# Reordering work at the group boundary of a fused linear-attention and gated-MLP kernel: one pair fetched per period, Erf behind the mean, the x split in two pieces, weights' parts behind the copy of k^T v

## The chip, the cores and the metric

The kernel runs on one core of a Trainium2 chip. The metric is the device time of one execution in microseconds (us); the kernel before takes 943.47 us (median of three runs, 943.17 to 945.06). A profiled execution of it spans 943.4 us, so times read in the trace can be compared with the metric directly.

## The reference, cut to what matters

```python
# q, k, v: (8, 8, 576, 64); w_in: (512, 2048); w_out: (2048, 512)
kv  = einsum('bhsd,bhse->bhde', k, v)             # k^T v, 64x64 for each head
out = einsum('bhsd,bhde->bhse', q, kv)            # linear attention, no softmax
rms = sqrt(mean(out * out, axis=-1) + 1e-6)
x   = (out / rms * g_norm) -> (4608, 512)         # tokens x (heads * head_dim)
h   = x @ w_in                                    # 4608 x 2048
g   = h * erf(softplus(h))
y   = g @ w_out                                   # 4608 x 512
```

## The kernel before

**Tiles and stages.** The 4608 tokens are worked in nine groups T of 512: the first 512 rows of each of the eight batches (T = 0 to 7), and the 64 rows left of each of the eight as group 8. The 2048 hidden columns are 16 units of 128, and four units make a *period*; a group has four periods, b = 0 to 3. Groups 0 and 1 form a first stage in which the weights are also converted and cut into parts. From group 2 on, the loop over m (line 1007) runs the periods, with T, b = divmod(m, 4).

**What a product is.** From group 2 on both matrix products work on numbers cut in parts: a rounded upper part, the remainder, and a scaled combination of both. `product` (line 663) therefore issues 12 matmuls of 128x512 for one result: eight into the bank `n_ps` (for each of four blocks k, the upper form and then the lower one) and four into the bank `m_ps`. The two banks are joined when they are read: ScalarE copies `n_ps` scaled into `h` (line 1057), then VectorE adds `m_ps` (line 649). `pair_of_banks` hands out three pairs of banks in turn, so a product waits until the product three before it has been read.

**A period.** In order: four `hidden` products u0 to u3 (x times w_in, for the units of this period), then four `result` products r0 to r3 (g times w_out, for the gate values of the period before; one for each 128 tokens). Around them stand the gate's steps. ScalarE takes Softplus of each `h` (line 1072), then Erf of two halves (line 1078); VectorE multiplies h by it (line 1101); in the next period ScalarE makes the upper part of g (`cut_upper`, which is line 609 in the profile) and VectorE the two lower ones (`cut_lower`, lines 612 and 615). VectorE also adds each result into `e` (lines 644 and 649).

**Attention in between.** While period (T, b) runs, the attention of group T+1 is worked for head pair p = b. `attention` returns it as a list of pieces, and the tuple `places` (lines 1022 to 1031) says where each is issued: 0 is the period's start, 1 to 4 come after u0 to u3, 5 to 8 after r0 to r3. The pieces of a group above 2 (`fused`) are: a first one, empty but for one pair; `visit` with `halve` and `keep_tail`; `loads`; `mean`; `norm`; `split`.

- `visit` (459): TensorE multiplies q by k^T v, and also turns q and works k^T v of the *next* pair; ScalarE squares the result (492) and copies the turned q (344, in `turned`); `tails_kept` (352) copies the last rows of q on VectorE (358) for every second pair; `halve` (517) cuts the squares in two; `keep_tail` keeps the last rows (498) and, by `kv_kept`, k^T v (364 and 371).
- `mean` (524): two pairs of short matmuls (537 and 538), then Ln, Exp and Square on ScalarE (552 to 554). They need another activation table than Softplus and Erf, so they bring a table load.
- `norm` (558): three VectorE operations (560, 563, 572) that give x.
- `split` (581): the upper part of x on ScalarE (609), the two others on VectorE (612 and 615), into `x_forms`, which u0 of the next group reads.
- `loads` (585): q, k and v of a later pair, through the queue of SyncE, into a pool of two buffers for each. In a fused group it fetches the pair three ahead, whose buffers are the ones that this visit has just read; the first fused visit fetches two pairs.

The engines take their work in the order of the code. At the *turn* of a group (b = 3) the last pair's `split` must be done before u0 of the next group can end: the last two of u0's eight `n_ps` matmuls read it.

**The weights.** The parts of w_in and w_out lie in device memory and are streamed in again for each group, 768 KB a unit (`load_parts`, line 801), through the same SyncE queue. `FETCH` (line 1004) gives the places of these loads; w_in has four buffers, so a load waits for the unit four before it. In the first stage `w_upper` and `w_lower` (lines 682 and 698) cut the weights; `w_lower` runs two VectorE operations for each unit at the head of a step (lines 876 and 877), and `keep_prepared`, which brings k^T v of the prepared pair from its bank to `bd_kv` (364 and 371), comes after it, in `steps[f + 1][0]`.

Of the kernel before, what the change touches and what calls it, by code (L numbers as in the profile page):

```python
# [43 lines left out]
AF = mybir.ActivationFunctionType  # L44
# [16 lines left out]
def kernel(  # L61
# [200 lines left out]
    def weights():  # L262

        w_next("split")
        w_next("join")
        w_next("load")
# [126 lines left out]
    def keep_prepared():  # L393
        kept.pop()()

    def attention(T, p, pools=None):

        st = {}

# [59 lines left out]
        def visit():  # L459


            qT, tail = ready.pop((T, p))
            at = st["at"] = at_tile()
            x = halves_of(qT)
            for a, i, o in ((0, 0, 0), (0, 1, 1), (1, 0, 1), (1, 1, 0)):
                nc.tensor.matmul(  # L466
                    at[rows_of[o], a, 0 : 2 * P],
                    lhsT=bd[rows_of[i], a * D : a * D + D],
                    rhs=x[rows_of[i], a],
                    start=True,  # L470
                    stop=True,
                )
            for s in rows_of:
                nc.tensor.matmul(
                    at[s, 0, 2 * P : 2 * P + R], lhsT=bd[s, 0:D], rhs=tail[s], start=True, stop=True
                )
            st["o"] = at[:, :, 0 : 2 * P]
            st["next"] = fused and then[0] < B
            if st["next"]:
                ps = pair_of_banks("q0_ps", "q1_ps")  # L480
                kvs = list(kv_products(*then, at, crossed=True))
                turns = list(turn_products(*then, ps))
                while kvs or turns:
                    for some in (turns, kvs):
                        for product_ in some[:4]:
                            product_()  # L486
                        del some[:4]
            if fused:
                st["sq"] = x_new.tile([P, G], FP32, name="sq", tag="x")
            else:  # L490
                st["sq"] = qT
            nc.scalar.activation(two(st["sq"]), st["o"], AF.Square)
            if st["next"]:
                qT = turned(*then, ps)
                tails_kept(*then, ps, qT)

        def keep_tail():
            nc.vector.tensor_copy(
                out=x_last[:, p, T * R : T * R + R], in_=st["at"][:, 0, 2 * P : 2 * P + R]
            )  # L500
            if st["next"]:
                kv_kept(*then, st["at"])

        def apply():
# [53 lines left out]
        def norm():  # L558
# [19 lines left out]
                op1=ALU.mult,  # L578
            )

        def split():
            if T >= FIRST:
                thirds(st.pop("x"), *(form[:, p] for form in x_forms[T]))

        def loads():
            if not fused or (T, p) == (FIRST + 1, 0):
                load_pair(T * NP + p + 2)
            if fused:
                load_pair(T * NP + p + 3)

        if T == 0:
            return products, apply, halve, mean, norm
# [8 lines left out]
            pieces = ((prepare_,), (visit,), (halve, keep_tail, loads))  # L601
        else:
            pieces = ((prepare_, loads), (visit,), (keep_tail,))
        return (*(partial(chain, *group) for group in pieces), mean, norm, split)


    def upper(x, high):
# [20 lines left out]
    def thirds(x, high, low, both):  # L628
        upper(x, high)
        lower(x, high, low, both)  # L630
# [182 lines left out]
    def pieces_of(T):  # L813


        steps = [([], [], []) for _ in range(FC)]
        for p in range(NP):
            products, apply, halve, mean, norm, split = attention(T, p)
            f = (BATCH - 1) * (p + 1) if T < FIRST else BATCH * p

            steps[f][2 if T == FIRST or p == 1 else 1].append(products)
            steps[f + 1][0].append(keep_prepared)
            steps[f + 1][1].append(apply)
            steps[f + 2][0].append(halve)
            with_erf = (f + 2) % BATCH == BATCH - 1

            place = 2 if T < FIRST and p == 0 else 1
            steps[f + 2][place].append(partial(mean, table=not with_erf))
            steps[f + 3][0].append(norm)
            steps[min(f + 4, FC - 1)][0].append(split)  # L830
        return steps
# [27 lines left out]
    for n in range(FIRST * FC + 1):  # L859
# [10 lines left out]
        if T < FIRST:  # L870
            if f == 0:
                steps = pieces_of(T + 1)

            if due(0 if n == 2 * (BATCH - 1) else 1):
                weights()
            for key in list(w_new)[:2]:
                w_lower(*key)
            for piece in steps[f][0]:
                piece()
# [127 lines left out]
    for m in range(first_batch, batches + 1):  # L1007
        T, b = divmod(m, NB)
        todo = []
        if T + 1 < NG:  # L1010
            todo = list(attention(T + 1, b))
            if b == 0:
                side = late_r if T % 2 == FIRST % 2 else late
                forms = side.tile([P, 3, KC, G], FP32R, name=f"x_forms{(T + 1) % 2}")
                x_forms[T + 1] = [forms[:, i] for i in range(3)]

        def piece():
            if todo:
                todo.pop(0)()


        places = (0, 2, 3, 5, 6, 8)
        if T + 1 == B:
            places = (0, 0, 0, 5, 6, 7)
            if b == NB - 1:


                places, todo[3] = (0, 0, 0, 4, 6, 7), partial(todo[3], table=False)
                todo[5] = partial(chain, todo[5], softplus_table)
        elif b == NB - 1:  # L1030
            places = (0, 2, 3, 5, 6, 7)

        def pieces(place):
            while todo and places[-len(todo)] <= place:
                todo.pop(0)()

        def fetch(place):
            for which in FETCH[place].split():
                load_parts(which, 1)


        to_last = m == B * NB - 1
        pieces(0)
        g, done = g_next, len(g_next)
        g_next = []
        if m < batches:

            pool, tag = (acc, "e") if m % 2 else (wide, "b")
            h = pool.tile([P, BATCH, G], FP32, name="h", tag=tag)
            s = gate_r.tile([P, BATCH, G], FP32, name="s", tag="s")  # L1050
        for i in range(BATCH):
            if m < batches:
                n_ps, m_ps = hidden(T, b * BATCH + i)
            fetch(i)

            def evacuate():
                nc.scalar.activation(h[:, i], n_ps, AF.Copy, scale=SHIFT - 1.0)  # L1057
                add(h[:, i], m_ps)


            early_copy = i == 0 and m == B * NB
            if early_copy:
                evacuate()
            if i == 0:
                for half in range(done, 2):
                    g.append(cut_upper(old_h, half))
            if i == 0 and not done:
                cut_lower(old_h, 0, g[0])
            if m < batches:
                if not early_copy:  # L1070
                    evacuate()
                nc.scalar.activation(s[:, i], h[:, i], AF.Softplus)  # L1072
            if i == BATCH - 1:
                cut_lower(old_h, 1, g[1])
            pieces(i + 1)
        if m < batches:
            for i in range(2):
                nc.scalar.activation(part(s, i), part(s, i), AF.Erf)  # L1078
            if len(todo) < 2:
                softplus_table()  # L1080
        T2, b2 = divmod(m - 1, NB)
        w = [w_now["out", b2 * BATCH + f].pop(0).bitcast(FP32R) for f in range(BATCH)]
        for j in range(J):
            cuts = 2 if m == batches and j == J - 1 else 1
            result(T2, b2, j, g, w, cuts)
            fetch(BATCH + j)
            if b2 == NB - 1:
                e = es.pop(j)
                if cuts == 1:
                    store(T2, j, e)  # L1090
            if j == 1 and m == batches - 1:
                cut_lower(h, 0, g_next[0])

            if m >= batches - 1:
                due_halves = (j,) if j < 2 and m < batches else ()
            else:
                due_halves = range(2) if j == (2 if to_last else 1) else ()
            if to_last:
                pieces(BATCH + 1 + j)
            for half in due_halves:  # L1100
                nc.vector.tensor_tensor(  # L1101
                    out=part(h, half), in0=part(h, half), in1=part(s, half), op=ALU.mult
                )
            if j == 0 and m == batches - 1:
                g_next.append(cut_upper(h, 0))
            pieces(BATCH + 1 + j)
        old_h = h
# [33 lines left out]
```

## Time and profile before

| what | value |
|---|---|
| time, median of 3 | 943.47 us |
| span of the profiled execution | 943.4 us |
| TensorE matmul busy | 920.1 us (98%) |
| VectorE busy | 728.8 us (77%) |
| ScalarE busy | 603.1 us (64%) |
| moved by DMA | 259.99 MB, mean 276 GB/s |
| a product of 12 matmuls, start to start | 2.72 us |
| a period in groups 3 to 6 | 24.3 to 24.4 us; 25.1 to 25.7 us where it begins at a turn |

Busy time of a matmul is a modelled span: one 128x512 matmul is shown with about 390 ns while the next starts 227 ns after it. So small stalls vanish inside busy time, and the distance from one product's start to the next is the better measure of what TensorE loses. An idle time stands in the profile with what ended it, the releaser.

### The profile page before, as it was taken

What the parts mean: (1) busy time and instruction counts of PE and PEld (TensorE: products, weight loads), DVE (VectorE), ACT (ScalarE), POOL (GpSimd) and SP (SyncE); (2) the same over time, 40 slices, a digit from 0 to 9 for tenths busy, and PEclk for the clock granted to TensorE, in tenths of its full rate; (3) what the DMA queues carried; (4) which work ended last, traced back from release to release, by engine and by line L of the source; (5) the groups of instructions that cost most, each with busy time, mean ns of one, the idle gap of its engine ahead of it and who ended that gap; (6) DMA issues with size and microseconds to landing.
All of it is one profiled execution on the core that took longest, in us unless ns stands there. A gap on an engine that the chain in (4) does not pass through costs nothing.

```text
span 943.4 us, 15388 instructions
## 1 busy us (share of the span) xinstructions
PE 920.1 (98%) x5998; PEld 685.3 (73%) x5998; DVE 728.8 (77%) x1074; ACT 603.1 (64%) x830; POOL 2.4 (0%) x10
## 2 busy tenths in 40 slices
PE   6999999999999999999999999999999999999998
PEld 4444445565687887888788878887888788888886
DVE  2788848788576888888878887888888878776677
ACT  3877666677665666666656666666666666665552
POOL 1000000000000000000000000000000000000000
PEclk9999999999999999999999999999999999999999
DMA  9866406888589998899888988998877678778872
GB/s 258 287 209 205 135 1 253 322 342 333 200 288 333 330 335 296 289 321 329 272 296 311 320 290 303 333 309 278 284 318 261 247 264 342 275 281 324 321 271 56
DMA packets 108271, 259.99 MB, mean 276 GB/s; under 512 B 43992, under 2 KB 66856, under 8 KB 108200
## 3 DMA queue, kind: packets, MB, share of 16 engines
q1 hardware_dynamic: 106488, 256.73, 76.8%
q10 hardware_dynamic: 1648, 2.29, 0.8%
q8 instruction: 47, 0.77, 0.3%
q14 instruction: 24, 0.20, 0.1%
q0 software_dynamic: 64, 0.00, 0.0%
HBM read 224.40 MB, written 34.60 MB: 275 GB/s over the span
## 4 chain that ended last, share of the span: by engine, by line
PE 71%; DVE 16%; ACT 6%; DMA 4%; issue 2%; SPq 0%; DVEq 0%; ACTq 0%
PE n_ps L671 35%; PE m_ps L671 17%; PE o_ps L727 8%; PE h_ps L907 4%; DVE e L649 3%; DVE h L1101 2%; DVE e L644 2%; DVE h L649 2%; PE at_ps L466 1%; DVE g_forms L612 1%; DMA w_in_parts<-w_in 1%; PE at_ps L486 1%; DMA k_sb<-in_k_dram 1%; DVE x L572 1%; DVE u L563 1%
## 5 line engine op out<-in xcount | busy, mean ns | idle before, releaser
L671 PE MATMUL n_ps<-x_forms,w_in_parts 128*128 128x512 f32 x896 | 227.8, 395 | 6.2 <-DVE x_forms L612 3.9
L671 PE MATMUL n_ps<-w_out_parts,g_forms 128*128 128x512 f32 x928 | 232.0, 392 | 0.0
L671 PEld LDWEIGHTS n_ps<-w_out_parts,g_forms 128*128 128x128 f32 x928 | 172.9, 188 | 37.1 <-issue 1.9
L671 PEld LDWEIGHTS n_ps<-x_forms,w_in_parts 128*128 128x128 f32 x896 | 167.1, 188 | 45.0 <-DVE x_forms L612 5.6
L1072 ACT ACTIVATE s<-h 128x512 f32<-128x512 f32 x112 | 70.8, 632 | 190.4 <-DVE h L649 190.3
L649 DVE TENSOR_TENSOR h<-m_ps,h 128x512 f32<-128x512 f32 x116 | 79.9, 689 | 90.8 <-ACT h L1057 60.3
L671 PE MATMUL m_ps<-w_out_parts,g_forms 128*128 128x512 f32 (+1 forms) x468 | 124.3, 388 | 0.0
L671 PE MATMUL m_ps<-x_forms,w_in_parts 128*128 128x512 f32 x448 | 120.5, 391 | 0.0
L727 PE MATMUL o_ps<-w_out_sb,h_sb 128*128 128x512 f32 x224 | 101.8, 597 | 0.2 <-DVE h_sb L857 0.2
L671 PEld LDWEIGHTS m_ps<-w_out_parts,g_forms 128*128 128x128 f32 x468 | 87.5, 188 | 18.5
L671 PEld LDWEIGHTS m_ps<-x_forms,w_in_parts 128*128 128x128 f32 x448 | 84.7, 189 | 17.8
L649 DVE TENSOR_TENSOR e<-m_ps,e 128x512 f32<-128x512 f32 (+1 forms) x117 | 80.3, 687 | 14.5 <-PE m_ps L671 3.8
L727 PEld LDWEIGHTS o_ps<-w_out_sb,h_sb 128*128 128x128 f32 x224 | 41.4, 190 | 44.8 <-issue 42.2
L1057 ACT ACTIVATE h<-n_ps 128x512 f32<-128x512 f32 x112 | 66.1, 590 | 10.4 <-PE n_ps L671 10.2
L615 DVE SCALAR_TENSOR_TENSOR g_forms<-g_forms 128x1024 fp32r<-128x1024 f32 x58 | 71.1, 1225 | 2.0
L612 DVE TENSOR_TENSOR g_forms<-h,g_forms 128x1024 fp32r<-128x1024 f32 x58 | 70.5, 1216 | 0.1
L609 ACT ACTIVATE g_forms<-h 128x1024 fp32r<-128x1024 f32 x58 | 58.4, 1048 | 15.1 <-PE m_ps L671 11.1
L1101 DVE TENSOR_TENSOR h<-h,s 128x1024 f32<-128x1024 f32 x56 | 65.9, 1216 | 0.0
L907 PE MATMUL h_ps<-xT,w_in_sb 128*128 128x512 f32 x144 | 64.8, 596 | 0.5 <-DVE w_in_sb L245 0.5
L644 DVE SCALAR_TENSOR_TENSOR e<-n_ps,e 128x512 f32<-128x512 f32 x88 | 60.1, 683 | 3.5 <-PE n_ps L671 3.5
L108 ACT ACT_TABLE_LOAD x44 | 56.5, 1283 | 0.7
L1078 ACT ACTIVATE s<-s 128x1024 f32<-128x1024 f32 x56 | 56.3, 1053 | 0.3
(128 smaller groups left out, 1023.4 us busy)
## 6 DMA issues: line engine op xcount, KB each, us to landing
w_out_parts<-w_out SPq DMA_DIRECT2D x116, 768.0 KB
w_in_parts<-w_in SPq DMA_DIRECT2D x112, 768.0 KB
w_in<-w_new SPq DMA_DIRECT2D x16, 768.0 KB
q_sb<-in_q_dram SPq DMA_DIRECT2D x32, 256.0 KB
w_raw<-in_moe_w_in_dram SPq DMA_DIRECT2D x16, 512.0 KB
w_raw<-in_moe_w_out_dram SPq DMA_DIRECT2D x8, 1024.0 KB
out_dram<-e SPq DMA_DIRECT2D x32, 256.0 KB
k_sb<-in_k_dram SPq DMA_DIRECT2D x28, 287.5 KB
```

The source lines that it names most:

```text
L108: nc.scalar.preload_act_table_set("softplus")
L609: nc.scalar.activation(high, x, AF.Copy, scale=1.0 + 2.0**-13)
L612: nc.vector.tensor_tensor(out=low, in0=x, in1=high.bitcast(FP32), op=ALU.subtract)
L615: nc.vector.scalar_tensor_tensor(out=both, in0=low.bitcast(FP32), scalar=SHIFT, in1=high.bitcast(FP32), op0=ALU.mult, op1=ALU.add,)
L644: nc.vector.scalar_tensor_tensor(out=out_, in0=ps, scalar=scale, in1=out_, op0=ALU.mult, op1=ALU.add)
L649: nc.vector.tensor_tensor(out=out_, in0=ps, in1=out_, op=ALU.add)
L671: nc.tensor.matmul(ps[:, cols], lhsT=weights(form, k), rhs=moving(form, k)[:, cols], start=(form == forms[0] and k == 0), stop=(form == fo ...
L727: nc.tensor.matmul(o_ps[j], lhsT=g[:, j * P : j * P + P], rhs=w_out_sb[:, f, :], start=(f == 0), stop=last,)
L907: nc.tensor.matmul(plain[i], lhsT=w_in_sb[:, i % FC, c], rhs=xT[T][:, c, :], start=(c == 0), stop=(c == KC - 1),)
L1057: nc.scalar.activation(h[:, i], n_ps, AF.Copy, scale=SHIFT - 1.0)
L1072: nc.scalar.activation(s[:, i], h[:, i], AF.Softplus)
L1101: nc.vector.tensor_tensor(out=part(h, half), in0=part(h, half), in1=part(s, half), op=ALU.mult)
```

## The change

The diff has four parts.

1. *One pair fetched per period.* `loads` fetches the pair two ahead, never three, and the first fused visit no longer fetches two pairs. Its target buffers are those of the visit before, so the load need not wait for the matmuls just issued.
2. *The turn of a group* (b = 3, five times). `mean` moves from after r0 to before Erf (place 4), without a table load of its own for Softplus; only the first half's Erf comes right after it, the second half's Erf and the Softplus table come after r0; `norm` moves from place 6 to 5; `split` is cut into `split_upper` (place 5) and `split_lower` (place 6); the product h times s moves from r1 to r2. At the first period of each group from 3 on, the copy of u0 from its banks comes ahead of `cut_upper` and `cut_lower` (before, only in group 8).
3. *The tails of q behind halve.* `tails_kept` moves from `visit` into `keep_tail`.
4. *Weights' parts behind k^T v's copy.* In the first stage `keep_prepared` runs ahead of `w_lower`.

```diff
@@ attention @@
             nc.scalar.activation(two(st["sq"]), st["o"], AF.Square)
             if st["next"]:
-                qT = turned(*then, ps)
-                tails_kept(*then, ps, qT)
+                st["turned"] = ps, turned(*then, ps)
         def keep_tail():
             ...
-            if st["next"]:
+            if st.get("next"):
+                tails_kept(*then, *st.pop("turned"))
                 kv_kept(*then, st["at"])
...
+        def split_upper():
+            if T >= FIRST:
+                upper(st["x"], x_forms[T][0][:, p])
+
+        def split_lower():
+            if T >= FIRST:
+                lower(st.pop("x"), *(form[:, p] for form in x_forms[T]))
+
         def split():
-            if T >= FIRST:
-                thirds(st.pop("x"), *(form[:, p] for form in x_forms[T]))
+            split_upper()
+            split_lower()
         def loads():
-            if not fused or (T, p) == (FIRST + 1, 0):
-                load_pair(T * NP + p + 2)
-            if fused:
-                load_pair(T * NP + p + 3)
+            load_pair(T * NP + p + 2)
...
+        after = (split_upper, split_lower) if in_parts else (split,)
+        return (*(partial(chain, *group) for group in pieces), mean, norm, *after)
@@ pieces_of and the first stage's loop @@
-            steps[f + 1][0].append(keep_prepared)
...
+            while kept:
+                keep_prepared()
             for key in list(w_new)[:2]:
                 w_lower(*key)
@@ the loop over periods @@
+        turn = b == NB - 1 and T + 1 < B
...
-        elif b == NB - 1:
-            places = (0, 2, 3, 5, 6, 7)
+        elif turn:
+            places, todo[3] = (0, 2, 3, 4, 5, 5, 6), partial(todo[3], table=False)
...
-            early_copy = i == 0 and m == B * NB
+            early_copy = i == 0 and b == 0 and first_batch < m < batches
...
-            for i in range(2):
+            for i in range(1 if turn else 2):
                 nc.scalar.activation(part(s, i), part(s, i), AF.Erf)
...
-                due_halves = range(2) if j == (2 if to_last else 1) else ()
-            if to_last:
+                due_halves = range(2) if j == (2 if to_last or turn else 1) else ()
+            if to_last or turn:
                 pieces(BATCH + 1 + j)
+            if turn and j == 0:
+                nc.scalar.activation(part(s, 1), part(s, 1), AF.Erf)
+                softplus_table()
```

More of the change, by code (lines that the diff above doesn't have):

```diff
@@ L394, in keep_prepared, with attention @@
         kept.pop()()
-    def attention(T, p, pools=None):
+    def attention(T, p, pools=None, in_parts=False):
         st = {}
@@ L603, in attention @@
             pieces = ((prepare_, loads), (visit,), (keep_tail,))
-        return (*(partial(chain, *group) for group in pieces), mean, norm, split)
+        after = (split_upper, split_lower) if in_parts else (split,)
+        return (*(partial(chain, *group) for group in pieces), mean, norm, *after)
     def upper(x, high):
@@ L1009 @@
         todo = []
+        turn = b == NB - 1 and T + 1 < B
         if T + 1 < NG:
-            todo = list(attention(T + 1, b))
+            todo = list(attention(T + 1, b, in_parts=turn))
             if b == 0:
```

## The prediction

> **What bounds the kernel now.** I read the page's busy times and chain first, then TensorE's waits, then the timeline around each long wait.
>
> ```profile
> PE 920.1 (98%) x5998; PEld 685.3 (73%) x5998; DVE 728.8 (77%) x1074; ACT 603.1 (64%) x830; POOL 2.4 (0%) x10
> PE 71%; DVE 16%; ACT 6%; DMA 4%; issue 2%; SPq 0%; DVEq 0%; ACTq 0%
> ```
>
> TensorE (PE) is the bound, and 16% of the chain passing through VectorE (DVE) says that some hand-overs to it are tight. Only what TensorE waits for can be won. Of its waits after the start-up, these three matter (total us, times, longest):
>
> ```profile
> PE n_ps L671 <- DVE x_forms L612: 3.9, 5, 0.8
> PE n_ps L671 <- DMA w_in_parts<-w_in: 1.9, 1, 1.9
> PE at_ps L466 <- DVE bd_kv L364: 1.6, 1, 1.6
> ```
>
> The change's parts 2, 1 and 4 aim at exactly these. Recorded idle understates them, since modelled matmul ends cover small gaps, so I size each by starts of products.
>
> *Wait A, the turn.* TensorE at the turn into group 4:
>
> ```profile
> 453.60 2.02 PE L671 MATMUL n_ps<-x_forms,w_in_parts 128*128 128x512 f32 x7
> 456.44 0.50 PE L671 MATMUL n_ps<-x_forms,w_in_parts 128*128 128x512 f32 x1 [0.82 <-DVE x_forms L612]
> 457.73 2.00 PE L671 MATMUL n_ps<-x_forms,w_in_parts 128*128 128x512 f32 x8
> ```
>
> u0 starts at 453.60, u1 at 457.73: 4.13 us where a product takes 2.72. VectorE and ScalarE (ACT) meanwhile:
>
> ```profile
> 449.94 2.35 DVE L1101 TENSOR_TENSOR h<-h,s 128x1024 f32<-128x1024 f32 x2
> 452.21 0.68 DVE L560 SCALAR_TENSOR_TENSOR u<-at_ps,u 128x512 f32<-128x512 f32 x1
> 455.71 0.68 DVE L612 TENSOR_TENSOR x_forms<-x,x_forms 128x512 fp32r<-128x512 f32 x1
> ```
>
> ```profile
> 448.84 1.28 ACT L105 ACT_TABLE_LOAD   x1
> 451.53 0.64 ACT L554 ACTIVATE u<-rms_r 128x512 f32<-128x512 f32 x1
> 452.18 1.28 ACT L108 ACT_TABLE_LOAD   x1
> 454.43 0.63 ACT L609 ACTIVATE x_forms<-x 128x512 fp32r<-128x512 f32 x1 [0.97 <-DVE x L572]
> ```
>
> The norm stands behind the gate's product (L1101, 2.35 us) and behind ScalarE's Erf and two table loads; the split's L612 ends at 456.39, while TensorE wanted it at about 453.60 + 7 x 0.227 = 455.19.
>
> *Wait B, the parts of w_in in the first fused group.* TensorE, then the same stretch in windows (the column after the last pair of brackets is the granted clock), then SyncE's queue:
>
> ```profile
> 290.84 3.14 PE L671 MATMUL n_ps<-x_forms,w_in_parts 128*128 128x512 f32 x8 [1.93 <-DMA w_in_parts<-w_in]
> ```
>
> ```profile
> 290.84:295.26 4.42, 4.42 (x12) 3.48 (x13) 0.69 (x1) 1.23 (x2) 0.00 (x0) 0.61 1.05 404
> ```
>
> ```profile
> 269.57 0.66 SPq L129 DMA_DIRECT2D q_sb<-in_q_dram  x1
> 275.95 0.40 SPq L809 DMA_DIRECT2D w_out_parts<-w_out  x1
> 279.26 0.43 SPq L809 DMA_DIRECT2D w_in_parts<-w_in  x1
> ```
>
> The second of the two pairs holds the queue from 269.57 to 275.95; the weights behind it go out late, and the load issued at 279.26 lands at 290.7. The wait is paid twice: the product after it runs at a clock of 0.61 and takes 4.42 us.
>
> *Wait C, k^T v in the first stage.* VectorE:
>
> ```profile
> 172.49 0.68 DVE L636 SCALAR_TENSOR_TENSOR w_new<-w_new,w_out_sb 128x512 fp32r<-128x512 f32 x1
> 174.53 0.69 DVE L639 TENSOR_TENSOR w_new<-w_new 128x512 fp32r<-128x512 f32 x1
> 175.14 0.28 DVE L364 TENSOR_REDUCE bd_kv<-at_ps 128x64 f32<-128x128 f32 x1
> ```
>
> Four operations on weights' parts (172.49 to 175.14) stand ahead of the reduce for which TensorE stops.
>
> [...]
>
> **Part by part.**
>
> *Part 2, the turn.* What it can remove: u0 to u2 takes 7.28 us in an undisturbed period with the same visit (503.69 to 510.97). At the turns it takes 8.19, 8.71, 8.70 and 8.63, so 0.91 + 1.43 + 1.42 + 1.35 = 5.11. At the last turn, which has no visit, 6.95 against 2 x 2.72 = 5.44: 1.51. Together 6.62 us over five turns.
>
> Does it? I lay the new order on the turn into group 4 with the durations of the rows. ScalarE: Softplus of u3 ends at 445.50; table 1.28, Ln 0.69, Exp 0.63, Square 0.64 end at 448.8; Erf's table 1.28 to 450.1, first Erf 1.0 to 451.1. The number of table loads stays at three. VectorE: after `cut_lower` and r0's additions at about 448.5 it waits 0.3 us for the Square, then the norm's 0.68 + 0.69 + 0.75 gives x at 451.05. Upper part of x on ScalarE to 451.8, then the second Erf (1.0) and the table (1.28) to 454.1. VectorE adds r1 to 452.4, splits x to 453.75. L612 is thus ready at about 453.1 against a need at 455.19: 2 us to spare, so the wait goes.
>
> What is pushed back: r2's additions end at 455.15, h times s at 457.4, r3's additions at 458.8. The banks of r1, r2, r3 are wanted by u0 at 453.6, u1 at 456.3 and the visit's turned q at about 459.6; they are free at 452.4, 455.15 and 458.8, spare 1.2, 1.2 and 0.8. At the last turn u2 wants r3's banks 5.44 after u0's start and they are free about 5.2 after: spare 0.2, the thinnest. Then u0's addition: behind `cut_lower` it would end near 462, too late for u2 at 460.9; with the early copy it ends at 459.5. That is the use of the early copy; it puts `cut_lower` 0.7 us later, and r0 reads that only after 466. `mean` before r0 adds no matmul; it needs `halve` 2.7 us earlier, and at the first such turn VectorE is done at 343.54 while u3's matmuls last to 343.96. Here a wait is added in TensorE's order, with all of r0 behind it; spare 0.4, more with part 3. I take 6.6, and 3.3 as the low end.
>
> *Part 3.* In every second visit VectorE waits 1.4 us for ScalarE's copies of q before it may start `halve`; now `halve` fills it. VectorE is not what TensorE waits for there: nothing on the path, only slack.
>
> *Part 1.* u2 at 285.95 to r0 at 295.26 is 9.31 us; the same stretch two periods on, 338.36 to 343.96, is 5.60. It loses 3.71. Without the second pair the w_out load goes out at about 269.6 in place of 275.95. The late w_in stands behind a store that waits for r1's additions (273.7), so it goes at about 274.2, 5 us sooner; it took 11.4 us to land behind a full queue, so at worst 285.7, and TensorE wants it at about 288.7. In later groups the same load has 14.4 us (376.45 for 390.81) with one pair a period, and no wait is seen. What is added: a pair now has one period, not two. The tightest issue is at b = 1: the last transfer goes out by 396 and the next visit comes at 410.5, 14 us later; the DMA is busy only 0.72 to 0.74 from 394 to 398, so it lands well before. I take 3.7; the low end is 0.
>
> *Part 4.* From the start of u's `m_ps` to L466 it is 2.73 us here and 1.03 at the next visit (202.55 to 203.58): 1.70. L466 to the next L727 is 1.01 against 0.69 because L371 is late too: 0.32. Reduce and copies take 0.28 + 0.39 us; put ahead they run from 172.5 to 173.2, before TensorE's arrival at 173.8. `w_lower` moves 0.7 us back, and its parts are read a step later, some 6 us. I take 2.0.
>
> Sum: 6.6 + 3.7 + 2.0 = 12.3. I leave 0.2 for the thin spots: 943.47 - 12.1 = 931.4.
>
> **Rivals.** *Turn only half won*: the bank waits or `mean` take its place. For it: spares of 0.2 and 0.4 in a pencil schedule; against: VectorE is 77% busy and idles 1.2 us in each of several later additions, so it catches up. 931.4 + 3.3 = 934.7. *The DMA wait moves*: a pair or a weight comes late once, with the clock's fall: 931.4 + 3.7 = 935.1. For it: the DMA runs at 410 to 430 GB/s after such bursts; against: the 14 us. *Slower*: fetching one period ahead is late once in each of groups 3 to 7, about 5 x 3.7 = 18.5: 949.9. For it: one landing did take 11.4 us; against: that load had two pairs ahead of it, and now no pair load waits on the visit's matmuls.
>
> **How the numbers follow.** All won 0.72; turn half won 0.13; DMA wait moves 0.07; slower 0.06; 0.02 between them and no change. The likeliest gives 931.4. The range ends at 930.0 (spread of runs, and a small wait of 0.3 at 285.95 gone too) and at 935.5, just above the two middle cases. Faster 0.92, same 0.02, slower 0.06.
>
> **What would show it.** After: no wait of n_ps on x_forms L612, on w_in_parts, or of L466 on bd_kv; u0 to u2 about 7.3 us at turns; clock 1.00 near 290; VectorE's and ScalarE's busy times as before. It is wrong if TensorE waits on h L649 or e L649 after a turn, on `sq_lo` before r0, or on k, v or q in a visit.

## The result, and the profile after

The changed kernel takes 934.88 us (median of 4 runs, 934.53 to 935.04) against 944.03 for the kernel before: a ratio of 0.9902, with a 95% interval of 0.9885 to 0.9919, that is 9.2 us less. A second set of runs gave 934.70 against 943.84 (0.9903). The forecast was 931.4 with a range of 930.0 to 935.5: the direction holds and the time lies in the range, but 3 of the 12.1 us that were forecast did not come. Of the kernel with part 4 for two head pairs only (below), one run of four took 1883.14 us, twice the others, for a reason that the record does not show, and is left out of the comparisons.

The profiled execution spans 932.8 us. Busy times and the chain, as on the page:

```profile
PE 916.4 (98%) x5998; PEld 684.5 (73%) x5998; DVE 728.5 (78%) x1074; ACT 603.4 (65%) x830; POOL 2.4 (0%) x10
PE 94%; ACT 2%; DVE 2%; DMA 1%; issue 0%; DVEq 0%; ACTq 0%
```

VectorE and ScalarE do the same work as before (728.5 and 603.4 us); the chain passes through TensorE for 94% in place of 71%. TensorE's waits after the start-up no longer hold any of the three, but two new ones (total us, times, longest):

```profile
PE at_ps L537 <- ACT w_new L639: 0.8, 1, 0.8
PE at_ps L537 <- DVE x_last L497: 0.5, 1, 0.5
```

**The turn.** TensorE at the turn into group 4, then VectorE, then ScalarE (line numbers are those of the changed kernel: the split's rows are 615, 618 and 621, h times s is 1114):

```profile
448.69 1.98 PE L677 MATMUL n_ps<-x_forms,w_in_parts 128*128 128x512 f32 x8
451.41 1.98 PE L677 MATMUL n_ps<-x_forms,w_in_parts 128*128 128x512 f32 x8
```

```profile
443.20 0.69 DVE L560 SCALAR_TENSOR_TENSOR u<-at_ps,u 128x512 f32<-128x512 f32 x1 [0.24 <-ACT u L554]
446.71 0.68 DVE L618 TENSOR_TENSOR x_forms<-x,x_forms 128x512 fp32r<-128x512 f32 x1
449.43 2.35 DVE L1114 TENSOR_TENSOR h<-h,s 128x1024 f32<-128x1024 f32 x2
```

```profile
442.53 0.63 ACT L554 ACTIVATE u<-rms_r 128x512 f32<-128x512 f32 x1
445.44 0.63 ACT L615 ACTIVATE x_forms<-x 128x512 fp32r<-128x512 f32 x1
```

u1 starts 2.72 us after u0: no stall. The norm (L560) now starts 5.5 us before u0, where it had started 1.4 before; it no longer stands behind h times s, and the split's L618 ends 1.3 us before u0 begins.

**The first fused group.** The stretch in windows, and SyncE's queue:

```profile
288.50:291.30 2.80, 2.80 (x15) 2.29 (x13) 2.60 (x9) 0.87 (x4) 0.00 (x0) 1.00 0.97 346
```

```profile
269.20 0.41 SPq L815 DMA_DIRECT2D w_out_parts<-w_out  x1
274.22 0.38 SPq L815 DMA_DIRECT2D w_in_parts<-w_in  x1
```

TensorE is busy without a gap at clock 1.00, and the two weight loads leave at 269.20 and 274.22 in place of 275.95 and 279.26; the forecast had 269.6 and 274.2.

**The first stage.** VectorE around the reduce for which TensorE had stopped, and the same reduce's neighbour, the copy of q's tails, for head pairs 0 and 2:

```profile
172.95 0.28 DVE L364 TENSOR_REDUCE bd_kv<-at_ps 128x64 f32<-128x128 f32 x1
```

```profile
143.11 0.36 DVE L358 COPY qT_last<-at_ps 128x64 f32<-128x64 f32 x2 [2.18 <-ACT qT L346]
```

```profile
200.30 0.36 DVE L358 COPY qT_last<-at_ps 128x64 f32<-128x64 f32 x2 [1.62 <-ACT qT L346]
```

Pair 1's reduce comes at 172.95 in place of 175.14, and L466 no longer waits. But for pairs 0 and 2 VectorE now stands still for 2.2 and 1.6 us until ScalarE has copied q, with `w_lower` queued behind it. At pair 0, `w_lower` starts at 140.89 in the trace of before and at 144.12 after, behind the copy that waits: VectorE kept to the order of the code here, with 2.2 us free.

**Where the time went.** I lay the two traces side by side by the starts of the products. From u0 of the first period (m = 8) to the last product the kernel before takes 10.68 us more: 6.6 at the five turns and 4.0 in the period after the first fused visit. That u0 starts at 253.88 before and at 253.92 after: the whole stage ahead of it, with wait C in it, brought nothing. And 10.7 is more than the 9.15 of the medians, because the profiled run of the kernel before took 945.18 us, 1.2 above its median of 944.03, and that of the changed kernel 934.53, 0.3 below its own. (A trace's span is 1.7 to 2.1 us shorter than the time of the same run, in every run here. So the span of 943.4 us, which looks like the median of 943.47, is that of a long run.)

The start of u0 holds the start-up, and that differs from trace to trace: the first `h_ps` matmul starts at 27.68 to 28.95 us in the 14 traces, at 28.05 and 28.94 in two of the changed kernel. From the second group of `o_ps` matmuls, results of the first stage (59.25 before, 59.22 after), to u0 it is 194.63 us before and 194.70 after, so part 4 brought nothing by this measure either.

### The profile page after: what moved, and what is told of

Its sections match the earlier page's. It is cut to its first block, busy times and chain, and to the rows that moved or that the text cites. A ratio compares the mean times of both kernels' runs of the same rounds, so it can differ in the third digit from the quotient of the medians.

```text
span 932.8 us, 15394 instructions
## 1 busy us (share of the span) xinstructions
PE 916.4 (98%) x5998; PEld 684.5 (73%) x5998; DVE 728.5 (78%) x1074; ACT 603.4 (65%) x830; POOL 2.4 (0%) x10
## 4 chain that ended last, share of the span: by engine, by line
PE 94%; ACT 2%; DVE 2%; DMA 1%; issue 0%; DVEq 0%; ACTq 0%
PE n_ps L677 47%; PE m_ps L677 23%; PE o_ps L733 9%; PE h_ps L914 6%; PE at_ps L466 2%; PE at_ps L486 1%; PE q_ps L486 1%; PE at_ps L380 1%; PE at_ps L537 1%; PE at_ps L538 1%; PE ms_ps L543 1%; PE at_ps L382 1%; DMA v_sb<-in_v_dram 1%; DMA q_sb<-in_q_dram 1%; DVE w_new L645 0%
## 5 line engine op out<-in xcount | busy, mean ns | idle before, releaser
L677 PE MATMUL n_ps<-x_forms,w_in_parts 128*128 128x512 f32 x896 | 224.2, 392 | 0.0
L618 DVE TENSOR_TENSOR g_forms<-h,g_forms 128x1024 fp32r<-128x1024 f32 x58 | 70.6, 1217 | 0.1
L615 ACT ACTIVATE g_forms<-h 128x1024 fp32r<-128x1024 f32 x58 | 58.4, 1050 | 15.1 <-PE m_ps L677 11.1
L1088 ACT ACTIVATE s<-s 128x1024 f32<-128x1024 f32 x51 | 51.5, 1054 | 0.3
```

What stands on the lines that cost most here:

```text
L615: nc.scalar.activation(high, x, AF.Copy, scale=1.0 + 2.0**-13)
L618: nc.vector.tensor_tensor(out=low, in0=x, in1=high.bitcast(FP32), op=ALU.subtract)
L677: nc.tensor.matmul(ps[:, cols], lhsT=weights(form, k), rhs=moving(form, k)[:, cols], start=(form == forms[0] and k == 0), stop=(form == fo ...
```

## The experiments

Each kernel was timed beside the kernel before on the same chip. The medians of the kernel before lie between 943.84 and 944.27 in these sets, so a difference between two kernels from different chips is uncertain by some 0.4 us. "Loss" below is the time from u0 of m = 8 to the last product, less the same in the changed kernel's trace, in which nothing is lost from there on.

**One pair a period alone**, on the kernel before:

```diff
-            if not fused or (T, p) == (FIRST + 1, 0):
-                load_pair(T * NP + p + 2)
-            if fused:
-                load_pair(T * NP + p + 3)
+            load_pair(T * NP + p + 2)
```

> The kernel before with part 1 alone (every loads fetches the pair two ahead). If the second pair in the queue is the cause of wait B: the wait of n_ps on w_in_parts near 290 us and the slow clock behind it go, about 3.7 us less than before, no wait on k, v or q in any visit. If the w_in load were late for another reason (the queue full anyway): no change, or the wait only moves, 0 to -1 us.

Measured 942.23 against 943.89, ratio 0.9979 (0.9972 to 0.9987): 1.7 us less, where 3.7 were expected. Its waits of TensorE that are of the kind looked for:

```profile
PE n_ps L668 <- DVE x_forms L609: 4.1, 5, 0.8
PE at_ps L466 <- DVE bd_kv L364: 1.6, 1, 1.6
```

The wait on w_in is gone and no visit waits on q, k or v: the cause is the second pair. The size is off, for two reasons. The first turn now loses 1.37 us where the trace before had 0.91 (0.94 in the trace of part 4 alone, which has the stall too; as I read it, the stall let VectorE catch up), so 0.46 is given back; the other reason shows two experiments on.

**The turn alone**, that is part 2 with `loads`, `tails_kept` and `keep_prepared` as before:

```diff
+            places, todo[3] = (0, 2, 3, 4, 5, 5, 6), partial(todo[3], table=False)
+            early_copy = i == 0 and b == 0 and first_batch < m < batches
```

> The kernel before with part 2 alone (the turn's order and the early copy). If the turn's loss is the x split arriving late: 6.6 us less than before, u0 to u2 at the five turns back to about 7.3 us. If VectorE as a whole is what the turn lacks, the wait comes back on the banks (h L649 or e L649): at most 3.3 us less.

Measured 938.86, ratio 0.9945 (0.993 to 0.996): 5.0 us less by the medians. In the trace no turn loses anything: u0 to u2 is 7.28 at the four turns with a visit and 5.44 at the last. Of its waits in the fused groups these are left:

```profile
PE n_ps L680 <- DMA w_in_parts<-w_in: 1.5, 1, 1.5
PE at_ps L537 <- DVE x_last L498: 0.3, 1, 0.3
```

What is left of loss, 2.5 us, is the wait on w_in (2.0 by starts of products) and 0.5 where mean's matmuls wait at m = 27, the last turn; the forecast had named this place as thin, at the first turn. So the late split is the cause, and VectorE has room for the new order. The timed gain lies below the 6.6 of the turns, which lies at the far end of the interval (0.7% of 943.89 is 6.6); the runs of this kernel spread from 937.33 to 941.78, and the trace's u0 of m = 8 comes 1.0 us later than before because its start-up is 1.2 us longer.

**Two pairs again, in the changed kernel** (part 1 taken back), the size of wait B in place:

> The changed kernel without part 1 (the first fused visit fetches two pairs again, later ones the pair three ahead). If wait B costs what it did in the profile of before: 3.7 us more than the changed kernel, all of it in the period after the first fused visit. If that profile had caught a long one: 1.5 to 2.5 us more, as in the trace of the turn alone (2.0).

Measured 937.45, ratio 0.9927 (0.991 to 0.9944): 2.6 to 2.8 us above the changed kernel, its runs from 935.88 to 940.05. The changed kernel's lie within 0.9 us. The trace is of a run of 939.16, and loses 3.7 us in this period, in several waits. TensorE there, and the clock in the windows:

```profile
292.51 2.06 PE L680 MATMUL n_ps<-x_forms,w_in_parts 128*128 128x512 f32 x8 [1.97 <-DMA w_in_parts<-w_in]
295.31 1.52 PE L680 MATMUL n_ps<-w_out_parts,g_forms 128*128 128x512 f32 x6
```

```profile
291.00:296.00 5.00, 3.49 (x16) 2.93 (x17) 1.46 (x4) 1.23 (x2) 0.00 (x0) 1.00 1.09 405
```

The stall is 1.97 us, as long as the 1.93 before; but the product behind it takes 2.80 us, not 4.42, and the clock stays at 1.00. Of the five traces that hold this wait (before, the turn alone, the tails alone, part 4 alone, this one; stalls of 1.3 to 2.0 us) only the first shows the product behind it slowed, by 1.70. That slow clock is what made wait B 3.7 us in that trace.

It is not the only way to such a loss. The trace of part 4 alone loses 3.7 us in this period at full clock, as TensorE waits for w_in twice:

```profile
287.36 2.09 PE L671 MATMUL n_ps<-x_forms,w_in_parts 128*128 128x512 f32 x8 [1.15 <-DMA w_in_parts<-w_in]
```

The five traces lose 4.0, 2.0, 1.7, 3.7 and 3.7 us here, and the time of the profiled run stands 1.2 above, 0.8 and 0.5 below, 1.6 and 1.7 above the median of its kernel. The loss less that excess is 2.0 to 2.9 us in all five: an estimate of what wait B costs in a usual run. How often the clock falls can be estimated from the runs, since each has its mean granted clock on record and the fall in the trace of before brings it to 0.998: of 101 runs of the kernels that fetch two pairs, 10 have 0.998 or 0.997; of 59 runs of the others none is below 0.999. In the kernel before these are 6 of 63, with a median of 945.84 us against 943.84 for the rest.

**The tails alone**, part 3 on the kernel before:

```diff
-                qT = turned(*then, ps)
-                tails_kept(*then, ps, qT)
+                st["turned"] = ps, turned(*then, ps)
...
+                tails_kept(*then, *st.pop("turned"))
                 kv_kept(*then, st["at"])
```

> The kernel before with part 3 alone (tails_kept behind halve). VectorE's idle of about 1.4 us before the tails' copy goes, TensorE waits for nothing of it: within 0.5 us of before. If that slack reached TensorE: 1 us or more less.

Measured 939.66, ratio 0.9951 (0.994 to 0.9963): 4.2 us less. The expectation of no change falls. Its waits of TensorE at the turns, and VectorE at the turn into group 4, where u0 starts at 450.84:

```profile
PE n_ps L671 <- DVE x_forms L612: 1.5, 5, 0.4
```

```profile
452.13 0.68 DVE L612 TENSOR_TENSOR x_forms<-x,x_forms 128x512 fp32r<-128x512 f32 x1
```

The wait of the turn shrinks from 3.9 to 1.5 us. In the kernel before, L612 starts 2.11 us after u0; here 1.29. VectorE arrives at the turn 0.8 us earlier, because the 1.4 us that it lost before the tails' copy in the visit of the same period are now filled. By starts of products the turns lose 0.52 to 0.72 us each in place of 0.91 to 1.51, together about 2.9 in place of 6.6. So this slack is on the path, as long as the turn itself hangs on VectorE.

**Pair and tails**, parts 1 and 3 on the kernel before, with no change at the turn:

> The kernel before with parts 1 and 3 alone, no change at the turn. From the trace of part 3 alone: the turns lose 0.5 to 0.7 us each in place of 1.4, so about 6 us less than before, 2.5 to 3 us above the changed kernel. If part 3's gain came from the DMA wait and not from the turns: 2 to 3 us less than before.

Measured 938.24, ratio 0.993 (0.9917 to 0.9944): 6.0 us less, 3.4 above the changed kernel. The trace loses 0.62 us at each of four turns and 0.75 at the last, 3.3 in all and nothing else from u0 of m = 8 on. This is the first of the two expected cases, near both sizes. It also shows that in company with part 3 the new order of the turn is worth some 3.3 us, half of the 6.6.

**The changed kernel again, and without part 3** (tails copied in `visit`, ahead of `halve`), on one chip:

> The changed kernel itself, as the reference for the three runs beside it on the same chip: about 0.990 of before (934.9 us), mean's matmuls of head pairs 0 and 2 in the first stage waiting about 0.5 and 0.85 us.

> The changed kernel without part 3 (the tails copied in visit, ahead of halve). If part 3 and the turn's new order remove the same loss: within 0.7 us of the changed kernel, TensorE without a wait at the turns, at most 0.5 us where mean's matmuls wait for halve. If part 3 earns its 4 us on its own: about 4 us more.

Measured 934.70 (ratio 0.9903) and 934.86 (0.9907): no difference. With the new order at the turn, part 3's 4 us are not there to win; both remove the same loss.

**keep_prepared first, alone**, part 4 on the kernel before:

```diff
-            steps[f + 1][0].append(keep_prepared)
...
+            while kept:
+                keep_prepared()
             for key in list(w_new)[:2]:
                 w_lower(*key)
```

> The kernel before with part 4 alone (keep_prepared ahead of w_lower). By the prediction's step: 2.0 us less. By the reading of the trace after the change: VectorE now waits 2.2 us (head pair 0) and 1.6 us (pair 2) for ScalarE's copy of q with w_lower standing behind it, so the mean's matmuls of these two pairs wait 0.5 and 0.85 us, and the time is within 0.5 us of before.

Measured 943.72, ratio 0.9997 (0.999 to 1.0005): nothing. The forecast's 2.0 us do not come. In the changed kernel's trace, TensorE and the last VectorE operation that it waits for, at pair 2:

```profile
210.59 0.36 PE L537 MATMUL at_ps<-sq_hi,mean_w 128*128 128x256 f32 x1 [0.85 <-ACT w_new L639]
```

```profile
210.22 0.22 DVE L497 COPY x_last<-at_ps 128x64 f32<-128x64 f32 x1
```

L537 starts 0.15 us after the copy of the last rows ends. The line names ScalarE, but the w_new in question is another tile; by the times it is VectorE.

**Without part 4, and with it for pairs 1 and 3 only**, on the chip of the run "again":

```diff
+            odd = f // BATCH % 2 == 1
-            while kept:
+            while kept and odd:
                 keep_prepared()
             for key in list(w_new)[:2]:
                 w_lower(*key)
+            while kept:
+                keep_prepared()
```

> The changed kernel without part 4 (w_lower first, as before). If part 4 gives back all it takes: within 0.5 us of the changed kernel, with the 1.6 us wait of L466 on bd_kv back and no wait of mean's matmuls. By the prediction's step: 2.0 us more.

> The changed kernel, with keep_prepared ahead of w_lower only for head pairs 1 and 3, and behind it for pairs 0 and 2, whose copy has to wait for ScalarE. If w_lower standing behind that wait is what gave part 4's gain back: both waits of mean's matmuls in the first stage go, L466 still does not wait, 1.5 to 2 us less than the changed kernel. If VectorE has simply no room in the first stage: the wait turns up at another instruction, less than 0.5 us.

Measured 935.06 without it (0.9908), 0.4 above the changed kernel, and 933.29 with it for the odd pairs (0.9885, 0.9868 to 0.9901), 1.4 below. VectorE and TensorE at pair 2 of the second:

```profile
199.58 0.69 DVE L645 TENSOR_TENSOR w_new<-w_new 128x512 fp32r<-128x512 f32 x1
200.19 0.35 DVE L358 COPY qT_last<-at_ps 128x64 f32<-128x64 f32 x2
```

```profile
208.80 0.28 PE L537 MATMUL at_ps<-sq_hi,mean_w 128*128 128x256 f32 x1
```

`w_lower` runs while ScalarE copies q, the tails' copy finds its data ready, and mean's matmuls of pairs 0 and 2 do not wait (those of pair 1 wait 0.15); L466 does not either. u0 of m = 8 starts at 252.05, against 253.92 and 254.75 in the two traces of the changed kernel. From the second group of `o_ps` matmuls to u0, without the start-up, it is 193.05 us here, 194.70 and 194.65 in the changed kernel's traces and 194.70 without part 4: part 4 as a whole brings nothing, and for the odd pairs alone 1.6 us. The timed intervals overlap, so the traces, not the times, show that this order wins most of what part 4 was for. This is the fastest kernel of the study.

**Without the early copy**, in the changed kernel:

```diff
-            early_copy = i == 0 and b == 0 and first_batch < m < batches
+            early_copy = i == 0 and m == B * NB
```

> The changed kernel without the early copy at a group's first period (u0 is read behind cut_lower, as before). If the early copy is needed, as the prediction's schedule has it: u2 waits about 1.1 us for u0's banks at each of the first four turns, 3 to 5 us more. If VectorE catches up without it: within 0.5 us.

Measured 937.36, ratio 0.9921 (0.9908 to 0.9935): 2.5 to 2.7 us more. The size is nearly as expected, the place is not:

```profile
PE at_ps L537 <- DVE x_last L497: 1.4, 2, 0.9
PE at_ps L537 <- DVE bd_kv L364: 0.3, 2, 0.2
```

u2 waits nowhere. At the turn into group 4 here, VectorE's addition of u0 ends at 457.32, a microsecond after u2 has started at 456.33: u2 fills its `n_ps` bank first, which ScalarE had read by then, as u2 starts without a wait, and comes to its `m_ps` bank only 1.9 us later, at 458.27. What happens is that VectorE is still behind at the end of the group: the reduce of the visit ends 0.9 to 1.15 us before u3 is through (2.72 us after its start) in the periods m = 15, 19 and 23 of the changed kernel, and from 0.33 before to 0.18 after without the early copy. Mean's matmuls, which the new turn puts right behind u3, then wait. That the hand-overs with ScalarE in each period leave VectorE no room to catch up is my reading, and was not tried.

**The mean back behind r0**, in the changed kernel:

```diff
-            places, todo[3] = (0, 2, 3, 4, 5, 5, 6), partial(todo[3], table=False)
+            places = (0, 2, 3, 5, 6, 6, 6)
...
-            for i in range(1 if turn else 2):
+            for i in range(2):
...
-            if turn and j == 0:
-                nc.scalar.activation(part(s, 1), part(s, 1), AF.Erf)
-                softplus_table()
```

> The changed kernel with the turn's mean back behind r0 (place 5, both halves of Erf ahead of it, norm and both pieces of the split at place 6); h times s stays at r2. If Erf ahead of the mean is what made x late: x comes some 3 us later, L612 near u0's last matmuls, a wait of 0.5 to 1 us at each turn, 2 to 5 us more. If only the place of h times s mattered: within 0.5 us.

Measured 944.73, ratio 1.0004 (0.9996 to 1.0012): about 10 us more, all that the change had won. VectorE, then TensorE:

```profile
448.74 0.69 DVE L560 SCALAR_TENSOR_TENSOR u<-at_ps,u 128x512 f32<-128x512 f32 x1 [2.17 <-ACT u L554]
454.37 2.35 DVE L1111 TENSOR_TENSOR h<-h,s 128x1024 f32<-128x1024 f32 x2
```

```profile
458.17 0.33 PE L486 MATMUL q_ps<-ident,q_sb 64*64 64x64 f32 x3 [0.47 <-DVE e L655]
```

VectorE stands 2.17 us before the norm until ScalarE, which took both Erfs first, has its Square. r3's additions are late by that, the turned q waits for their banks, and each turn loses 1.65 to 2.3 us. This is more than the expected case, which had looked at x alone and forgotten what queues behind the standing VectorE. So the mean ahead of r0 and of the second Erf is what carries part 2. What the later place of h times s and the split in two pieces bring by themselves was not tried.

## Why the prediction was right or wrong

**How the time came to lie in the range.** In part by luck. The case that was forecast, all three waits won, would have given 931.4. The range went up to 935.5 for two rivals, a turn half won (934.7) and a DMA wait that moves (935.1). The measured 934.88 stands beside their numbers, but neither happened: no trace of the changed kernel shows a wait at a turn or for a load in a fused group. What is missing comes from two terms of the sum itself, parts 1 and 4.

**The turn: right, in mechanism and size.** No wait is left, and the two traces differ by 6.6 us there. The pencil schedule was on the safe side: L612 was to end 0.5 us before u0's start and ends 1.3 before; r3's additions were to end 5.2 us after it and end 4.5; mean's matmuls were to have 0.4 us and have 0.8 to 1.15 at the first four turns and 0.4 at the last. Two steps inside it were wrong without harm. "It would end near 462, too late for u2 at 460.9" took the two banks of a pair as one; the early copy is worth its 2.5 us by keeping VectorE ahead of mean's matmuls. And "so it catches up", said against the first rival, did not hold where it was tested: without the early copy VectorE was still late three periods on.

**The DMA wait: right in mechanism, mis-sized.** The term of 3.71 consisted of a wait (2.0) and of the slowed product behind it (1.70: the clock is 0.50 for 3.41 us of it). "The wait is paid twice" was read from one profiled run, and the run that it was read from took 945.18 us, 1.7 above the median of 943.47; in four other traces with the same wait the slowed product is not there, and about one run in ten (10 of 101) has the mean clock, 0.998 or 0.997, that would go with the fall. Taking part 1 back costs 2.6 us in the median and 1.0 to 5.2 us in single runs. So about 1.1 of the missing 3 us is here.

**k^T v's copy: wrong.** The step "I take 2.0" followed the reduce of head pair 1 alone. `keep_prepared` runs for each of the four pairs of group 2, and for pairs 0 and 2 it starts with the copy of q's tails, which waits for ScalarE. Moved ahead, this wait stops VectorE for 2.2 and 1.6 us with `w_lower` and then `halve` behind it; before, `w_lower` had filled the same time. Mean's matmuls lose what L466 had won: by the starts of the `o_ps` products around them, the stretch with pair 1's reduce is 1.70 us shorter after the change, and those with the mean's matmuls of pairs 0 and 2 are 0.67 and 1.08 us longer. "`w_lower` moves 0.7 us back" named what is queued behind the moved instructions, but not that they would wait. Measured: 0.2 us alone and 0.4 in place, both within the spread of the runs, and nothing by the traces; about 1.4 us more, and 1.6 by the traces, when applied to the odd pairs only. So nearly all of the 2.0 that were taken are missing.

**The tails: wrong alone, right in company.** "Nothing on the path, only slack" is right for the changed kernel (934.86 against 934.70). On the kernel before, the same edit brings 4.2 us, since the turn that the forecast had traced to VectorE's order hangs on how late VectorE arrives as well. The step asked who waits for VectorE at the visit, and not who waits for it later in the same period.

**The sum.** 6.6 for the turns, 2.6 for part 1 and nothing for part 4 make 9.2, against the measured 9.15. The slower rival (a pair one period ahead arriving late) did not come: no visit waits on q, k or v in any trace with part 1.

## What to carry to other kernels

- An instruction that is moved ahead in an engine's order takes its own wait with it: here VectorE stood for 2.2 and 1.6 us before the copies of q's tails, and `w_lower` did not go past them. Go through every place where it runs, not just the one that stalls, and see which of them has its data ready; put it first only there.
- A gain of two edits that relieve the same engine is not a sum. The parts brought 1.7, 5.0, 4.2 and 0.2 us alone, 11.1 together on paper, and 9.15 in fact; and what one piece of a part costs when taken back (10 us for the order of Erf and mean) can exceed what the whole part brings.
- Before a term is read from one trace, compare that run's time with the median. The traced run here was 1.2 to 1.7 us longer than the medians of its kernel, and its loss at wait B was that much above the usual one.

## What the runs showed of the hardware that was not expected

- A stall of TensorE of 1.9 to 2.0 us was followed by a half clock in one trace (granted 0.61 over 4.42 us) and by a full clock in another (1.00, the next product in 2.80 us). In the first, the clock is 1.00 over the stall (288.91 to 290.84) and until 291.57, 0.73 us after TensorE has work again, then 0.50 for 3.41 us, to 294.98, and 1.00 after that. Elsewhere in the same trace it stays at 1.00 around wait C (172 to 176, a wait of 1.6 us) and at the turn into group 4 (452 to 458, a wait of 0.82). What decides whether the clock falls was not tried.
- Where VectorE waits for it, its copy of q's tails starts 0.03 us after the end of ScalarE's copy from the same tile (143.11 after 143.08 in the first stage of the changed kernel, 288.52 after 288.49 in a fused group of the kernel before), although both only read. Whether the chip or the program's own semaphores ask for that was not tried.
